# V of every batch from float32 W1, and batch 2's x and half of its z turned by VectorE, in an attention and two-layer kernel on one core

## The chip, the cores and the metric

The program runs on one core of a Trainium2 chip. Its engines are TensorE (PE in the rows; PEld is its weight loads), VectorE (DVE), ScalarE (ACT) and GpSimd (POOL); SyncE (SP) only issues transfers here. The metric is the device time of one execution in microseconds, as the median of several.

## The reference

```python
# x: 8 batches, 8 heads, 512 tokens, 64;  state: 8, 8, 32, 64
xread = softmax(x @ state.T / 8) @ state      # every token reads the state
sread = softmax(state @ x.T / 8) @ x          # the state reads the tokens
a = concat([xread, sread], axis=2)            # 544 tokens of 512 for each batch, 4352 in all
h = a @ w_in                                  # 512 -> 1024
s = h * softmax(h)
z = (s - mean(s)) / sqrt(var(s) + 1e-6) * g_ln
y = z @ w_out                                 # 1024 -> 512
o = y @ w3
out = (o * sigmoid(1.702 * o)) @ w4           # 512 -> 2048 -> 512
```

## The kernel before, in words

**Stages.** The first stage, up to about 440 us, does the attention, the layer with softmax and norm, and w_out, for 8 batches of 512 tokens; the 256 tokens read by the states follow as a ninth, short batch. The second stage multiplies by w3, the third by w4, both in a seven-product block scheme, and together they last to the end.

**How a product is made exact enough.** Most products are three matmuls of rounded parts: high times high, high times low, low times high (`mm3`, L421 to L424, type float32r). A "split" of a tile writes its high part (a rounding copy, L457) and its low part (a subtraction, L458). A few products are single float32 matmuls: the transposes, the scores (L571), the reads (L633) and some of the V below (L671).

**V.** Instead of reading the state and then multiplying by w_in, the kernel multiplies the state of each batch by w_in first: V = state @ W1, four tiles of 128x512 in a batch (two groups g of four heads, two halves f of 1024 columns). The tokens of the batch then take attention weights times V (L763). Batches 0 and 1 make V in `state_w1`: for each tile two float32 matmuls, one for each pair of heads, each with 64 columns of the turned state `stT` as weights and 512 columns of W1 moving; ScalarE rounds the result (`vhi`, L675), VectorE subtracts (`vlo`, L676). Batches 2 to 7 are taken two at a time (`DIRECT`, `state_w1_both`): the states of a pair are split (`sthi`, `stlo`), and each of eight products with the split W1 (`W1s`, in the trace `hi_w1s`, `lo_w1s`) is three matmuls of 128 columns by 512. Its result holds half the rows of either batch's tile, so two copies of 64 rows (`v`, L711) bring these together, and `v` is split afterwards (`hi_v`, `lo_v`). So that the halves land on the right partitions, an odd batch of a pair has its two head pairs swapped (`turned`).

**Turning.** x and z have to be turned before they are multiplied. TensorE turns a 512x128 piece by four matmuls with the identity (`x_T`, L543; `z_T`, L827), and the result is copied out of PSUM. The other way is VectorE's transpose of 32x32 blocks, with transfers that put the blocks in place: for x the transfers come first (`x_T_dma`, L529, tile `xb`, then the transpose at L533), for z the transposes come first (`z_turn`, L797, tile `zw`, then the transfers at L806 into `z`). `XD` and `ZB` say from which batch on x, and the second half of z, go this way: both are 3.

**What sets the order.** The program lists steps with their inputs, outputs, a cost for each engine that may do it, and for TensorE a place in its order (`key`). A planner (`Plan.plan`) then goes through them in a modelled time and fixes the order on each engine, and which engine does a step where two may; rows of the program come out in that order, and each engine runs its own in order. Tiles of 128x512 words live in 71 shared slots of kind `s` (22 more from the point where the first stage's own tiles are done).

Of the kernel before, what the change touches and what calls it, by code (L numbers as in the profile page):

```python
# [19 lines left out]
NWIDE = 7  # L20
NRAW = 2
NZ = 2
ZB = 3
XD = 3
AHEAD = 30.092
KF = 11.222
LOOK = 27.436
KR = 1.553
DIRECT = 2
W1S = 20.477  # L30
ATT = -0.491
ZL = 7.738
M1B = -7.631
VST = 25.191
RK = 6
LEAD = 62.849
KEEP = 5
# [306 lines left out]
def attention_solu_gelu(ctx: ExitStack, tc: tile.TileContext, x, state, w1, w2, g_ln, w3, w4, out):  # L344
# [52 lines left out]
    def PE(c):  # L397
        return [("pe", c)]
# [105 lines left out]
    def attention(b):  # L504
# [5 lines left out]
            n_step[0] += 1  # L510
            return base + (n_step[0] - 1) * SLOT / steps[0]

        both = b >= DIRECT
        turned = both and b % 2
        xt = {}
        load_x(b, 0)
        if not turned:
            load_state(b)
        for j in range(1, NP):
            load_x(b, j)  # L520

# [43 lines left out]
        def scores(g):  # L565
            p = tl("m", [P, 512], F32, f"psc{b}_{g}")

            def go(e):
                for i in range(2):
                    jj = i ^ turned  # L570
                    e.matmul(p()[64 * i:64 * i + 64, :], stT[b]()[:, g, 64 * jj:64 * jj + 64], xt[2 * g + jj](),  # L571
                             start=True, stop=True)

            do(PE(.9), go, [stT[b], xt[2 * g], xt[2 * g + 1]], [p], key())
# [51 lines left out]
        def read_s():  # L626
            p = tl("m", [P, 512], F32, f"psr{b}")

            def go(e):
                for g in range(G):  # L630
                    for c in range(C):
                        for hl in range(HG):
                            e.matmul(p()[NS * hl:NS * hl + NS, g * D:(g + 1) * D],  # L633
                                     e2k[g]()[:, c, NS * hl:NS * hl + NS],
                                     xn[b, 2 * g + (hl // 2 ^ turned)]()[:, c, hl % 2, :],
                                     start=(c == 0), stop=(c == C - 1))

            do(PE(1.55), go, [e2k[0], e2k[1]] + [xn[b, j] for j in range(NP)], [p], key())
            sr = tl("t", [P, G, 2, D], F32, f"sr{b}")
            for g in range(G):  # L640
                do(DVE(.26), lambda e, g=g: e.tensor_scalar(
                    sr()[:, g], p()[:, g * D:(g + 1) * D].unsqueeze(1).to_broadcast([P, 2, D]),
                    r2[g]()[:, 1:2], None, op0=ALU.mult), [p, r2[g]], [sr])
            p2 = tl("m", [P, 512], F32, f"psrT{b}")

            def go2(e):
                for g in range(G):
                    e.transpose(p2()[:, g * P:(g + 1) * P], sr()[:, g].rearrange("p a d -> p (a d)"), ident)

            do(PE(.22), go2, [sr], [p2], key())  # L650
            for q in range(2):
                for a in range(2):
                    def go3(e, q=q, a=a):
                        pv = p2()[:, 0:G * P].rearrange("p (j a n) -> p j a n", a=2, n=NS)
                        o = xs[q]()[64 * a:64 * a + 64, :, b * NS:(b + 1) * NS]
                        if turned:
                            for j in range(2):
                                copy(e, o[:, j], pv[64 * a:64 * a + 64, 2 * q + 1 - j, a, :])
                        else:
                            copy(e, o, pv[64 * a:64 * a + 64, 2 * q:2 * q + 2, a, :])  # L660
                    c = 1 + bool(turned)
                    do([("act", .11 * c), ("dve", .13 * c)], go3, [p2], [xs[q]])

        def state_w1(g, f):
            p = tl("m", [P, 512], F32, f"pv{b}_{g}_{f}")
# [10 lines left out]
            do(DVE(.6), lambda e: e.tensor_tensor(lo(), p(), hi(), op=ALU.subtract), [p, hi], [lo])  # L676
            V[b, g, f] = (hi, lo)

        def state_w1_both():


            hi = tl("s", [P, G, 4, 64], F32R, f"sthi{b}")
            lo = tl("s", [P, G, 4, 64], F32R, f"stlo{b}")
            for i in range(2):
                st = stT[b + i]

                def part(t, i=i):
                    return t()[:, :, 1:3, :] if i else t()[:, :, 0:4:3, :]

                def src(st=st):  # L690
                    return st().rearrange("p g (j n) -> p g j n", j=2)

                do([("act", .29), ("dve", .2)], lambda e, part=part, src=src: copy(e, part(hi), src()), [st], [hi])
                do([("pool", .68), ("dve", .33)], lambda e, part=part, src=src: e.tensor_tensor(
                    part(lo), src(), part(hi), op=ALU.subtract), [st, hi], [lo])
            for f in range(2):
                for g in range(G):
                    v = [tl("s", [P, 512], F32, f"v{b + i}_{g}_{f}") for i in range(2)]
                    for jj in range(2):
                        p = tl("m", [P, 512], F32, f"pv{b}_{g}_{f}_{jj}")  # L700

                        def go(e, p=p, g=g, f=f, jj=jj):
                            wh, wl = W1s[2 * g + jj, f]
                            at = [t()[:, g, 2 * jj:2 * jj + 2, :].rearrange("p i n -> p (i n)") for t in (hi, lo)]
                            mm3(p(), *at, wh(), wl(), True, True)

                        do(PE(.65), go, [hi, lo, *W1s[2 * g + jj, f]], [p], key())
                        for side in range(2):
                            t = v[side ^ jj]
                            r = slice(64 * side, 64 * side + 64)  # L710
                            do([("act", .48), ("dve", .6)], lambda e, t=t, p=p, r=r: copy(e, t()[r, :], p()[r, :]),  # L711
                               [p], [t])
                    for i in range(2):
                        V[b + i, g, f] = split(v[i], f"v{b + i}_{g}_{f}", None)

        x_T(0)
        x_T(1)
        if not turned:
            state_T(b)
        e0 = scores(0)  # L720
        x_T(2)
        x_T(3)
        e2_T(0, e0)
        e1 = scores(1)
        n_step[0] += 1
        if both and not turned:
            load_state(b + 1)
            state_T(b + 1)
        e2_T(1, e1)
        read_s()  # L730
        if both and not turned:
            n_step[0] -= 1
            steps[0] = VST
            state_w1_both()
        if not both:
            for f in range(2):
                for g in range(G):
                    state_w1(g, f)


    n_tiles = {b: C for b in range(B)}
# [473 lines left out]
            prepare_up(k, q, (160, 230, 310)[n])  # L1215
    attention(0)
    for b in range(B):
        if b + 1 == DIRECT:
            for f in range(2):
                for k in range(KD):  # L1220
                    W1s[k, f] = split(W1[k, f], f"w1s_{k}_{f}", b * SLOT + W1S + 2 * (k + KD * f))
        if b + 1 < B:
            attention(b + 1)
        for i in range(C):
            step = SLOT / C if b < B - 1 else SLOT / 6
            last[b] = mlp1(b, i, b * SLOT + M1B + i * step if b else M1A + i * M1S)
        if b == B - 1:
            key = b * SLOT + C * SLOT / 6
            for j in range(KD // 2):
                xs2.append(split(xs[j], f"xs{j}", key - 3, (2, NX)))  # L1230
            for i in range(n_tiles[B]):
                last[B] = mlp1(B, i, b * SLOT + (C + i) * SLOT / 6)
# [77 lines left out]
```

## Time and profile before

| | |
|---|---|
| median of 3 runs | 1126.65 us (1126.53 to 1130.48) |
| the profiled execution | 1126.07 us |
| its span, first to last instruction | 1124.3 us |
| TensorE busy | 1080.0 us, 96% |
| VectorE busy | 825.2 us, 73% |
| ScalarE busy | 637.8 us, 57% |
| GpSimd busy | 258.7 us, 23% |
| mean granted TensorE clock | 0.992 |

The profiled execution is 1.8 us longer than its span and 0.6 us under the median. Matmuls are pipelined: the duration of a row runs on into the next matmul's, so what a matmul costs on TensorE is read from the distance of two starts.

### The profile page before, as it was taken

The page shows a single profiled execution, that of the slowest core. Times are in us where ns is not written, and L with a number is a line of the kernel's source. Part 1 is how long each engine was busy: PE and PEld are TensorE (multiplying, and loading weights), DVE is VectorE, ACT ScalarE, POOL GpSimd, SP SyncE. Part 2 cuts the span into 40 slices and gives each one's busy share as a digit, 9 for nine tenths or more (in the row PEclk, how much of TensorE's full clock was granted, in tenths as well). Part 3 has the DMA queues.
Part 4 walks back from the last instruction along what each step waited for, and adds up shares of the span by engine and source line. Part 5 has one row for each costly group of instructions (what it writes and reads, how often), then busy time and mean ns, then how long its engine had stood idle before and what let it go on. Part 6 is the DMA issues. An engine that isn't in the chain of part 4 may idle for free.

```text
span 1124.3 us, 21689 instructions
## 1 busy us (share of the span) xinstructions
PE 1080.0 (96%) x8055; PEld 976.9 (87%) x8055; DVE 825.2 (73%) x1398; ACT 637.8 (57%) x1171; POOL 258.7 (23%) x218
## 2 busy tenths in 40 slices
PE   6798999799899999999999999999999999999998
PEld 2466677577677889999999999999999999999998
DVE  6999878988989746628757755634388888788874
ACT  6686756866868546547666656545244444344341
POOL 3865443743746701301111000000000000000000
PEclk8899999999999999999999999999999999999999
DMA  8214234568673569998667657559944254344431
GB/s 242 67 39 113 78 70 135 165 126 177 187 162 87 158 153 365 334 374 276 230 233 242 237 204 257 179 209 398 383 145 125 64 170 150 101 144 151 134 93 57
DMA packets 233082, 202.78 MB, mean 180 GB/s; under 512 B 128784, under 2 KB 174864, under 8 KB 232976
## 3 DMA queue, kind: packets, MB, share of 16 engines
q1 hardware_dynamic: 232880, 201.26, 57.3%
q8 instruction: 63, 1.03, 0.4%
q14 instruction: 43, 0.35, 0.1%
q10 hardware_dynamic: 96, 0.13, 0.1%
HBM read 113.25 MB, written 82.84 MB: 174 GB/s over the span
## 4 chain that ended last, share of the span: by engine, by line
PE 75%; DVE 13%; issue 3%; SPq 3%; POOL 3%; DMA 2%; ACT 1%; DVEq 0%; POOLq 0%; ACTq 0%
PE psum L1098 9%; PE psum L1100 9%; PE psum L1099 9%; PE psum L1010 9%; PE psum L1011 9%; PE psum L1012 9%; PE psum L422 5%; PE psum L423 5%; PE psum L424 4%; DVE w_w L449 1%; DVE w_w L444 1%; SPq L529 1%; POOL lo_w3s L458 1%; DVE w_w L447 1%; DVE u L775 1%
## 5 line engine op out<-in xcount | busy, mean ns | idle before, releaser
L1098 PE MATMUL psum<-w4r,hi_g 128*128 128x256 f32 x896 | 251.8, 281 | 1.6 <-DVE oc L1109 1.6
L1100 PE MATMUL psum<-w4r,lo_g 128*128 128x256 f32 x896 | 251.6, 281 | 0.0
L1099 PE MATMUL psum<-w4r,hi_g 128*128 128x256 f32 x896 | 251.6, 281 | 0.0
L1098 PEld LDWEIGHTS psum<-w4r,hi_g 128*128 128x128 f32 x896 | 169.1, 189 | 1.8 <-ACT hi_g L463 1.8
L1100 PEld LDWEIGHTS psum<-w4r,lo_g 128*128 128x128 f32 x896 | 169.3, 189 | 0.0
L1099 PEld LDWEIGHTS psum<-w4r,hi_g 128*128 128x128 f32 x896 | 169.0, 189 | 0.0
L463 ACT CAST hi_g<-a_g 128x512 fp32r<-128x512 f32 x124 | 75.4, 620 | 127.3 <-DVE a_g L880 87.1
L451 POOL TENSOR_TENSOR w_w<-w_w,raw_w 128x512 uint32<-128x512 uint32 x48 | 68.9, 1441 | 284.1 <-DVE w_w L449 206.1
L1022 DVE TENSOR_TENSOR c<-psum,u 128x512 f32<-128x512 f32 x64 | 44.1, 689 | 98.0 <-PE psum L1012 63.7
L422 PE MATMUL psum<-zhi,hi_w 128*128 128x512 f32 (+1 forms) x288 | 113.9, 395 | 1.3 <-DVE zlo L835 0.6
L424 PE MATMUL psum<-zhi,lo_w 128*128 128x512 f32 (+1 forms) x288 | 109.9, 382 | 0.0
L957 DVE TENSOR_TENSOR lo_g<-a_g,hi_g 128x512 fp32r<-128x512 f32 x128 | 84.0, 685 | 19.9 <-PE psum L1099 7.1
L994 ACT ACTIVATE t<-c 128x512 f32<-128x512 f32 x96 | 60.5, 632 | 50.0 <-DVE c L1022 49.9
L957 DVE TENSOR_TENSOR lo_g<-gr,hi_g 128x512 fp32r<-128x512 f32 x104 | 71.0, 685 | 11.8 <-ACT hi_g L463 9.2
L423 PE MATMUL psum<-zlo,hi_w 128*128 128x512 f32 (+1 forms) x208 | 78.3, 376 | 0.2
L463 ACT CAST hi_g<-gr 128x512 fp32r<-128x512 f32 x104 | 61.8, 618 | 28.4 <-PE psum L1099 14.4
L422 PEld LDWEIGHTS psum<-zhi,hi_w 128*128 128x128 f32 x288 | 54.2, 188 | 17.3 <-issue 4.1
L424 PEld LDWEIGHTS psum<-zhi,lo_w 128*128 128x128 f32 x288 | 54.1, 188 | 11.8 <-DVE lo_w L458 0.4
L1010 PE MATMUL psum<-hi_x,w3r_1h 128*128 128x256 f32 x224 | 63.1, 282 | 1.2 <-ACT u L1017 1.2
L1011 PE MATMUL psum<-lo_x,w3r_2h 128*128 128x256 f32 x224 | 63.1, 282 | 0.0
L1010 PE MATMUL psum<-hi_x,w3r_2h 128*128 128x256 f32 x224 | 63.0, 281 | 0.0
L1011 PE MATMUL psum<-lo_x,w3r_3h 128*128 128x256 f32 x224 | 63.0, 281 | 0.0
(261 smaller groups left out, 3101.9 us busy)
## 6 DMA issues: line engine op xcount, KB each, us to landing
g<-t SPq DMA_DIRECT2D x136, 256.0 KB, 3.4
gr<-g SPq DMA_DIRECT2D x136, 256.0 KB, 3.4
w4r<-w4k SPq DMA_DIRECT2D x56, 256.0 KB, 5.2
raw_w<-in_moe_w_in SPq DMA_DIRECT2D x24, 512.0 KB, 6.0
raw_w<-in_moe_w_out SPq DMA_DIRECT2D x24, 512.0 KB, 4.2
xb<-scr SPq DMA_DIRECT2D x34, 256.0 KB, 6.3
scr<-x SPq DMA_DIRECT2D x16, 512.0 KB, 3.6
out<-oc SPq DMA_DIRECT2D x32, 256.0 KB, 3.8
```

What stands on the lines that cost most here:

```text
L422: nc.tensor.matmul(o, lhi, rhi, start=first, stop=False)
L423: nc.tensor.matmul(o, lhi, rlo, start=False, stop=False)
L424: nc.tensor.matmul(o, llo, rhi, start=False, stop=last)
L451: do(POOL(1.23), lambda e: e.tensor_tensor(u(), u(), raw()[:, :, 0], op=ALU.add), [w, raw], [w], key=due)
L463: e.copy(o, i)
L957: do(DVE(.68), lambda e: e.tensor_tensor(flat_(lo), flat_(t), flat_(hi), op=ALU.subtract), [t, hi], [lo], key=due)
L1010: nc.tensor.matmul(o, wh()[:, k, cut], hi()[:, k, :], start=first and not mi + k, stop=False, **OPEN)
L1011: nc.tensor.matmul(o, wh()[:, k, cut], lo()[:, k, :], start=False, stop=False, **OPEN)
L1012: nc.tensor.matmul(o, wl()[:, k, cut], hi()[:, k, :], start=False, stop=bool(mi and k), **OPEN)
L1098: nc.tensor.matmul(o, hi()[:, mi, cut], wt[:, 0], start=first, stop=False, **OPEN)
L1099: nc.tensor.matmul(o, hi()[:, mi, cut], wt[:, 1], start=False, stop=False, **OPEN)
L1100: nc.tensor.matmul(o, lo()[:, mi, cut], wt[:, 0], start=False, stop=2 * j + mi == NM - 1 and u == 1, **OPEN)
```

## The change

V of all batches is made by `state_w1`: two float32 matmuls for each tile, a rounding copy, a subtraction. `state_w1_both` and the swapping of head pairs go, and each batch loads and turns its own state. `XD` and `ZB` become 2, so the four pieces of batch 2's x, and the second half of its z, are turned by VectorE and transfers. The split of W1 into `W1s` is listed just ahead of batch 7 instead of ahead of batch 2's first half, with the due time that goes with it; the last, short batch (L754) still uses it.

```diff
-ZB = 3
-XD = 3
+ZB = 2
+XD = 2
...
-DIRECT = 2
...
-VST = 25.191
...
-        both = b >= DIRECT
-        turned = both and b % 2
...
-        if not turned:
-            load_state(b)
+        load_state(b)
...
-                    jj = i ^ turned
-                    e.matmul(p()[64 * i:64 * i + 64, :], stT[b]()[:, g, 64 * jj:64 * jj + 64], xt[2 * g + jj](),
+                    e.matmul(p()[64 * i:64 * i + 64, :], stT[b]()[:, g, 64 * i:64 * i + 64], xt[2 * g + i](),
...
-                        if turned:
-                            for j in range(2):
-                                copy(e, o[:, j], pv[64 * a:64 * a + 64, 2 * q + 1 - j, a, :])
-                        else:
-                            copy(e, o, pv[64 * a:64 * a + 64, 2 * q:2 * q + 2, a, :])
+                        copy(e, o, pv[64 * a:64 * a + 64, 2 * q:2 * q + 2, a, :])
...
-        def state_w1_both():
...
-        if not turned:
-            state_T(b)
+        state_T(b)
...
-        if both and not turned:
-            load_state(b + 1)
-            state_T(b + 1)
         e2_T(1, e1)
         read_s()
-        if both and not turned:
-            n_step[0] -= 1
-            steps[0] = VST
-            state_w1_both()
-        if not both:
-            for f in range(2):
-                for g in range(G):
-                    state_w1(g, f)
+        for f in range(2):
+            for g in range(G):
+                state_w1(g, f)
...
-        if b + 1 == DIRECT:
+        if b + 1 == B:
             for f in range(2):
                 for k in range(KD):
                     W1s[k, f] = split(W1[k, f], f"w1s_{k}_{f}", b * SLOT + W1S + 2 * (k + KD * f))
```

Line numbers of the changed kernel are lower: 671 becomes 660, 458 becomes 456, 676 becomes 665, 827 becomes 770. Three places show the order of the program's rows. The first is TensorE's, where the V of batch 2 begins, among the z products of batch 0 (`zhi`, `hi_w`) and transposes of its z (`u`). Before:

```order
L827 MATMUL psum<-ident,u_0_705 128x128
L827 MATMUL psum<-ident,u_1_732 128x128
L827 MATMUL psum<-ident,u_2_761 128x128
L827 MATMUL psum<-ident,u_3_814 128x128
L422 MATMUL psum<-hi_w1s_0_482,sthi_934 128x512
L423 MATMUL psum<-lo_w1s_0_604,sthi_934 128x512
L424 MATMUL psum<-hi_w1s_0_482,stlo_976 128x512
L422 MATMUL psum<-zhi_4_1022,hi_w_4_1162 128x512
```

And of the change (`stT_831` is batch 2's turned state, the four `w_w` are float32 tiles of W1):

```order
L660 MATMUL psum<-w_w_2_0_380,stT_831 64x512
L660 MATMUL psum<-w_w_3_0_384,stT_831 64x512
L770 MATMUL psum<-ident,u_0_917 128x128
L770 MATMUL psum<-ident,u_1_1008 128x128
L770 MATMUL psum<-ident,u_2_1040 128x128
L770 MATMUL psum<-ident,u_3_1253 128x128
L660 MATMUL psum<-w_w_0_1_401,stT_831 64x512
L660 MATMUL psum<-w_w_1_1_414,stT_831 64x512
```

Three float32r matmuls for half a tile of two batches have become pairs of float32 matmuls for a whole tile of one. The second place is VectorE's, where batch 2's V is finished; before, among the block transposes of batch 3's x (`xT`) and the softmax of batch 2 (`z_2_1`):

```order
L533 STREAM_TRANSPOSE xT_2_1314<-xb_2_1255 128x512
L465 CAST hi_v_0_0_1323<-v_0_0_1194 128x512
L600 TENSOR_REDUCE z_2_1_1325<-s_2_1_1103 128x16
L601 TENSOR_SCALAR z_2_1_1325<-z_2_1_1325 128x16
L602 RECIPROCAL z_2_1_1325<-z_2_1_1325 128x16
L780 TENSOR_SCALAR sml_3_1172<-sml_3_1172 128x1
L465 CAST hi_v_1_0_1341<-v_1_0_1281 128x512
L458 TENSOR_TENSOR lo_v_1_0_1344<-v_1_0_1281,hi_v_1_0_1341 128x512
```

And of the change:

```order
L528 STREAM_TRANSPOSE xT_3_1351<-xb_3_1321 128x512
L665 TENSOR_TENSOR vlo_0_0_1385<-psum,vhi_0_0_1379 128x512
L665 TENSOR_TENSOR vlo_1_0_1398<-psum,vhi_1_0_1391 128x512
L778 SCALAR_TENSOR_TENSOR zlo_0_1402<-psum,g_sb,zhi_0_1396 128x512
L665 TENSOR_TENSOR vlo_0_1_1410<-psum,vhi_0_1_1404 128x512
L665 TENSOR_TENSOR vlo_1_1_1419<-psum,vhi_1_1_1412 128x512
```

All four subtractions of a batch's V now stand on VectorE, with one input in PSUM. The third place is GpSimd's, in the first 60 us, where the low parts of W1 are made. Before:

```order
L458 TENSOR_TENSOR lo_w1s_0_536<-w_w_0_0_336,hi_w1s_0_479 128x512
L603 TENSOR_TENSOR s_0_1_393<-s_0_1_393,z_0_1_524 128x512
L451 TENSOR_TENSOR w_w_2_1_464<-w_w_2_1_464,raw_w_2_1_328 128x512
L451 TENSOR_TENSOR w_w_3_1_489<-w_w_3_1_489,raw_w_3_1_390 128x512
L610 TENSOR_TENSOR alo_1_584<-aT_1_565,ahi_1_571 128x512
L458 TENSOR_TENSOR lo_w1s_0_604<-w_w_1_0_360,hi_w1s_0_482 128x512
```

And of the change:

```order
L456 TENSOR_TENSOR lo_w1s_0_536<-w_w_0_0_336,hi_w1s_0_479 128x512
L597 TENSOR_TENSOR s_0_1_393<-s_0_1_393,z_0_1_524 128x512
L449 TENSOR_TENSOR w_w_2_1_464<-w_w_2_1_464,raw_w_2_1_328 128x512
L449 TENSOR_TENSOR w_w_3_1_489<-w_w_3_1_489,raw_w_3_1_390 128x512
L604 TENSOR_TENSOR alo_1_584<-aT_1_565,ahi_1_571 128x512
L456 TENSOR_TENSOR lo_w1s_0_604<-w_w_1_0_360,hi_w1s_0_482 128x512
```

Nothing moved here: the planner puts the split of W1 where it was, although the step is listed later.

## Rows read from the trace of the kernel before

**Rows 1.** Busy time by stretch: us, each engine (instructions), granted clock, DMA, GB/s

```profile
60.00:130.00 70.00, 62.27 (x346) 43.50 (x345) 66.52 (x123) 55.57 (x105) 42.47 (x38) 1.00 0.34 92
130.00:180.00 50.00, 49.43 (x296) 38.76 (x295) 34.93 (x67) 29.00 (x60) 15.93 (x16) 1.00 0.35 86
180.00:220.00 40.00, 35.59 (x221) 26.51 (x221) 39.08 (x70) 29.02 (x57) 26.68 (x23) 1.00 0.40 108
220.00:280.00 60.00, 57.40 (x326) 43.88 (x325) 48.62 (x91) 39.31 (x78) 26.64 (x24) 1.00 0.75 168
280.00:320.00 40.00, 34.60 (x216) 25.98 (x215) 38.26 (x63) 32.32 (x60) 25.89 (x21) 1.00 0.67 192
320.00:440.00 120.00, 119.84 (x658) 97.32 (x657) 83.02 (x146) 72.97 (x139) 46.23 (x39) 1.00 0.59 169
440.00:1124.00 684.00, 677.53 (x5725) 676.74 (x5723) 465.44 (x757) 340.37 (x600) 37.99 (x25) 1.00 0.61 206
```

**Rows 2.** Groups of TensorE's instructions, 0 to 440 us: busy, mean ns, idle before

```profile
L422 PE MATMUL psum<-hi_v,ahi 128*128 128x512 f32 x96 | 39.5, 411 | 3.4 <-DVE xs L465 2.6 <-DVE u L775 0.9
...
L422 PE MATMUL psum<-hi_w1s,sthi 128*128 128x512 f32 x24 | 11.0, 457 | 5.8 <-DVE zlo L835 2.5 <-DVE sr L641 2.1 <-ACT v L463 0.6
L621 PE MATMUL psum<-ident,e2t 128*128 128x128 f32 x64 | 10.4, 287 | 10.7 <-ACT e2t L583 10.7
```

**Rows 3.** TensorE's timeline, 59 to 65 us: start, length, line, tiles, count

```profile
59.34 1.08 PE L671 MATMUL psum<-w_w,stT 128*64 128x512 f32 x4
60.35 0.66 PE L543 MATMUL psum<-ident,xn 128*128 128x128 f32 x4
60.94 1.08 PE L671 MATMUL psum<-w_w,stT 128*64 128x512 f32 x4
61.95 0.44 PE L555 MATMUL psum<-ident,S 128*128 128x128 f32 x2
...
64.04 0.60 PE L543 MATMUL psum<-ident,xn 128*128 128x128 f32 x4
64.39 0.47 PE L422 MATMUL psum<-vhi,ahi 128*128 128x512 f32 x1
```

**Rows 4.** TensorE's timeline, 97 to 102 us

```profile
97.90 0.40 PE L422 MATMUL psum<-hi_w1s,sthi 128*128 128x512 f32 x1
...
98.60 0.39 PE L422 MATMUL psum<-zhi,hi_w 128*128 128x512 f32 x1
...
100.84 0.60 PE L827 MATMUL psum<-ident,u 128*128 128x128 f32 x4
101.20 0.48 PE L422 MATMUL psum<-hi_w1s,sthi 128*128 128x512 f32 x1
...
101.99 0.39 PE L422 MATMUL psum<-zhi,hi_w 128*128 128x512 f32 x1
```

**Rows 5.** Instructions of tiles vlo and v: shortest/median/longest ns, first and last start

```profile
L676 DVE TENSOR_TENSOR vlo<-psum,vhi x8: 645/684/693, 35.3 to 64.1; 128x512 fp32r<-128x512 f32 x8
...
L463 ACT COPY v<-psum x47: 562/581/592, 98.8 to 311.9; 64x512 f32<-64x512 f32 x47
...
L458 POOL TENSOR_TENSOR lo_v<-v,hi_v x17: 1272/1308/1762, 113.2 to 344.0; 128x512 fp32r<-128x512 f32 x17
L458 DVE TENSOR_TENSOR lo_v<-v,hi_v x7: 679/969/1783, 115.2 to 346.4; 128x512 fp32r<-128x512 f32 x7
L465 DVE CAST hi_v<-v x3: 379/417/1533, 112.7 to 308.4; 128x512 fp32r<-128x512 f32 x3
```

**Rows 6.** Groups of VectorE's instructions, 0 to 440 us

```profile
L797 DVE STREAM_TRANSPOSE zw<-u 128x512 f32<-128x512 f32 x20 | 13.8, 693 | 8.1 <-POOL u L786 5.4 <-DMA xn<-in_x 2.0 <-DMA z<-zw 0.7
L533 DVE STREAM_TRANSPOSE xT<-xb 128x512 f32<-128x512 f32 x20 | 13.4, 688 | 0.0
```

**Rows 7.** Instructions of tile lo_w1s, as in rows 5

```profile
L458 POOL TENSOR_TENSOR lo_w1s<-w_w,hi_w1s x8: 1287/1304/1478, 32.5 to 58.8; 128x512 fp32r<-128x512 f32 x8
```

**Rows 8.** SyncE's queue of transfers, 28 to 175 us: start, length, line, tiles, count

```profile
34.81 1.97 SPq L500 DMA_DIRECT2D S<-in_state  x4
75.91 12.02 SPq L436 DMA_DIRECT2D raw_w<-in_moe_w_out  x4
88.01 5.43 SPq L529 DMA_DIRECT2D xb<-in_x  x8
```

More of the change, by code (lines that the diff above doesn't have):

```diff
@@ L634, in go @@
                                      e2k[g]()[:, c, NS * hl:NS * hl + NS],
-                                     xn[b, 2 * g + (hl // 2 ^ turned)]()[:, c, hl % 2, :],
+                                     xn[b, 2 * g + hl // 2]()[:, c, hl % 2, :],
                                      start=(c == 0), stop=(c == C - 1))
@@ L655, in go3 @@
                         o = xs[q]()[64 * a:64 * a + 64, :, b * NS:(b + 1) * NS]
-                        if turned:
-                            for j in range(2):
-                                copy(e, o[:, j], pv[64 * a:64 * a + 64, 2 * q + 1 - j, a, :])
-                        else:
-                            copy(e, o, pv[64 * a:64 * a + 64, 2 * q:2 * q + 2, a, :])
-                    c = 1 + bool(turned)
-                    do([("act", .11 * c), ("dve", .13 * c)], go3, [p2], [xs[q]])
+                        copy(e, o, pv[64 * a:64 * a + 64, 2 * q:2 * q + 2, a, :])
+                    do([("act", .11), ("dve", .13)], go3, [p2], [xs[q]])
         def state_w1(g, f):
@@ L677, in state_w1 @@
             V[b, g, f] = (hi, lo)
-        def state_w1_both():
[L682 to L695, printed above, removed]
-            for f in range(2):
-                for g in range(G):
[L698 to L714, printed above, removed]
         x_T(0)
         x_T(1)
-        if not turned:
-            state_T(b)
+        state_T(b)
         e0 = scores(0)
@@ L725, in attention @@
         n_step[0] += 1
-        if both and not turned:
-            load_state(b + 1)
-            state_T(b + 1)
         e2_T(1, e1)
         read_s()
-        if both and not turned:
-            n_step[0] -= 1
-            steps[0] = VST
-            state_w1_both()
-        if not both:
-            for f in range(2):
-                for g in range(G):
-                    state_w1(g, f)
+        for f in range(2):
+            for g in range(G):
+                state_w1(g, f)
     n_tiles = {b: C for b in range(B)}
```

## The prediction

> **What bounds the kernel now.** I read the busy time by stretch first. From 320 us on TensorE is busy all the time: 119.84 of 120 us up to 440, then 677.53 of 684 [rows 1]. Nothing in those last two stages is edited, so the end comes when TensorE has got through the first stage. There it does wait: from 60 to 320 us the five stretches leave 7.7, 0.6, 4.4, 2.6 and 5.4 us idle, 20.7 together, and the large ones are those in which VectorE is full, 66.5 of 70, 39.1 of 40 and 38.3 of 40 us [rows 1]. The granted clock is 1.00 in each of them, its upper level, so a matmul's price doesn't change inside the part that is edited. The groups of TensorE's instructions then say where it waits: 10.7 us before the transposes of the exponentials, 5.8 before the products of W1's split halves with the states, 3.4 before the products that use the finished V of a pair [rows 2]. So the time is TensorE's work plus its waits in the first stage, and the change touches both.
>
> **The change on TensorE.** A float32 pair for one tile of V takes 1.01 us, from its start to that of the next instruction: 59.34 to 60.35 and 60.94 to 61.95 [rows 3]. Six batches (2 to 7) of four tiles make 24 pairs, 24.2 us. They replace 24 triples of float32r matmuls (three pairs of batches, eight products each). A triple takes 0.70 us among other triples, 97.90 to 98.60, and 0.79 behind transposes, 101.20 to 101.99 [rows 4]; so 16.8 to 19.0 us go, and I take 17.5. The same 0.09 us may now be paid by the triple behind each pair, 0 to 2.2 us; I take 1.1. V therefore adds 24.2 + 1.1 - 17.5 = 7.8 us, between 24.2 - 19.0 = 5.2 and 26.4 - 16.8 = 9.6.
>
> Batch 2's x no longer comes over TensorE: four groups of four transposes, each between 0.35 us (64.04 to 64.39) and 0.59 (60.35 to 60.94) [rows 3], 1.4 to 2.4 us, I take 1.9. Four groups of z transposes go too, 0.36 us each (100.84 to 101.20) and perhaps the 0.09 behind them [rows 4], 1.4 to 1.8 us, I take 1.6. TensorE's sum is 7.8 - 1.9 - 1.6 = +4.3 us, with bounds of 5.2 - 4.2 = +1.0 and 9.6 - 2.8 = +6.8.
>
> One rule speaks for a far larger price. The trace shows the two matmuls of a pair together in 1.01 us [rows 3], where one float32r matmul takes 0.70 / 3 = 0.23 [rows 4]. The Trainium skill, "FP8 and Floating Point Precision", section TensorE Precision Notes, says that true float32 makes four passes through the array. With four passes of 0.23 each and no overlap, 48 matmuls would cost 44.8 us and the sum would be 44.8 - 17.5 - 3.5 = +23.8 us, about 1150. The row disagrees with the second half of that: two matmuls of 64 columns share the time of one. I go by the row.
>
> **The change off TensorE.** VectorE gets 24 subtractions from PSUM at 0.684 us [rows 5], 16.4 us, four block transposes of x at 0.688 and four of z at 0.693 [rows 6], 5.5 us. It loses the seven `lo_v` it did, at a median of 0.97, and three `hi_v` at 0.42 [rows 5], 8.1 us. The order of the changed program also hands seven more two-input steps (low halves of weights, scalings of u) back to GpSimd, which has lost 17 `lo_v`; at `lo_v`'s 0.97 that is another 6.8 us. Net 21.9 - 8.1 - 6.8 = +7 us; with 0.68 to 1.78 for the fourteen steps that leave [rows 5] it is between -4 and +11. ScalarE loses 47 copies of 64 rows at 0.58 us [rows 5], 27 us, and GpSimd 17 times 1.31 [rows 5], 22 us, of which the seven come back. Neither is full in any stretch [rows 1], so this costs and gives nothing by itself; it counts through the waits.
>
> SyncE issues 32 more transfers, at 5.43 / 8 = 0.68 us each [rows 8], 22 us of its queue. Those of x stand, in the changed order, ahead of the third weight tile of w_out, for which the queue of before did nothing from 36.8 to 75.9 us [rows 8]: this gap hides them. Behind that wait, batch 2's x would come with what is now batch 3's at 88 us, some 20 us late, and its scores would be late next. The sixteen of z stand behind the stores of batch 1's result and ahead of w3's raw tiles and batch 5's x; 11 us of delay there meet nothing that TensorE needs within a batch. Price zero; cover as named.
>
> W1 is not split later, although the step is listed later: the order is the same, and the low halves are made at 32 to 60 us as now [rows 7]. So the 16 slots of W1's halves stay in use from there, and the 8 of float32 W1 stay too, until batch 7's V. This can delay only what waits for slots, the weights of the second stage. That stage waits 684 - 677.5 = 6.5 us in all now, and the 120 us before it hardly at all [rows 1]; so I take 0, with 0 to 3 (half of that stage's waits again) as bounds.
>
> **The waits.** Two things pull against each other. The V products no longer need a split state, two copies from two PSUM tiles and a split by GpSimd that takes at least 1.27 us [rows 5]; 5.8 + 3.4 = 9.2 us of TensorE's idle stand at such products now [rows 2]. Most of it ends on VectorE steps that stay (the low halves of z, the reads, copies), so I let half go: -4.6. Against it VectorE's +7 lies in a stage that has it full for 150 of 260 us [rows 1]; that share of it, 4.0 us, reaches TensorE. The sum is about nothing, with -9.2 (all such waits vanish) and +11 (all VectorE work is passed on) as bounds.
>
> So 1126.07 + 4.3 = 1130.4 against the profiled execution, which lies 0.6 under the median: **1131 us**.
>
> **Rivals.**
>
> The waits win. V's shorter way is worth the whole 9.2 us, and GpSimd's fewer steps speed VectorE up: `lo_v` there, with both inputs in SBUF, takes 0.68 to 1.78 us while `vlo`, with one input in PSUM, takes 0.645 to 0.693 [rows 5]. Some 15 fewer such steps on GpSimd at the 0.3 us between shortest and median give VectorE 4.5 us, of which 2.6 reach TensorE by the same share. 1126.65 + 4.3 - 9.2 - 2.6 = 1119. It is faster from 4.3 us of saved waits on, and measurably (0.5%, 5.6 us, is what this kernel's measurement can tell) from 9.9 on. The Trainium skill, "SBUF — State Buffer", section Who interferes with whom, says that a VectorE step with two SBUF inputs and a GpSimd step that reads SBUF lock each other out, and one with a single SBUF input doesn't; the spread of the two rows agrees. Against the rival stands that its waits end mostly on steps that stay. Chance 0.18.
>
> VectorE becomes the bound. Each batch's four subtractions stand in its queue in a block, each behind ScalarE's rounding, and what is queued behind them are the low halves of z and the row maxima for which TensorE and ScalarE wait. If all of the +7 to +11 reaches TensorE, the time is 1131 + 3 to 1131 + 11, some 1138 in the middle. For it speaks VectorE at 95 to 98% in three stretches; against it that ScalarE and GpSimd become lighter. The order is also made anew from batch 1 on, and a wait may open anywhere. Chance 0.25.
>
> The change holds more memory than it says, since W1's halves don't wait for batch 7: weights come late, +3, 1134. Chance 0.05, as the later stretches hardly wait now.
>
> Float32 pairs don't overlap among float32r products as they do among transposes: about 1150. Chance 0.02, since the rows of both kinds are at hand.
>
> **How the numbers follow.** The forecast (TensorE's sum, waits level, 1127 to 1135) has 0.5. Faster than 1121.0 takes about half of the first rival, 0.10. Slower than 1132.3 takes nearly all of the second, the two small ones and the forecast's upper quarter, 0.40; the rest, 0.50, lies within 0.5%. The range 1121 to 1141 leaves out the lower half of the first rival and the top of the second with the last.
>
> **What would show it.** TensorE's timeline should have 24 more float32 pairs at 1.01 us apart from the next start, between about 85 and 330 us, and no `sthi` products; the first stage should end some 4 us later, and the stretches after it be the same length. VectorE's busy time up to 440 us should be a few us higher, ScalarE's some 25 lower, GpSimd's some 15 to 20 lower. The idle before the V products should shrink, and idle before the products with zlo or the transposes of exponentials should grow by as much. The prediction is wrong if TensorE's idle from 60 to 320 us leaves 12 to 32 us, if a pair costs other than 1.0 to 1.1 us, or if waits appear behind 440 us.

## The result, and the profile after

The changed kernel takes **1133.22 us** (median of 6 runs, 1132.33 to 1134.39); the kernel before took 1125.68 us beside it (6 runs, 1123.66 to 1130.48). The ratio is 1.0063, with a 95% interval of 1.0042 to 1.0083. The forecast was 1131 with a range of 1121 to 1141; the time lies in the range, but the 0.63% is just past the 0.5% that bounded "no change": what came is "slower", to which the prediction gave 0.40, and not "within 0.5%", to which it gave 0.50. Of 31 more executions of the kernel before, the nine with a mean granted clock of 0.985 to 0.988 took 1129.2 to 1132.7 us, the others, with 0.989 to 0.992 as in the profiled one, 1124.7 to 1128.6. The profiled execution took 1132.84 us, its span is 1131.0, 6.7 more than before.

Busy time by stretch, in the columns and stretches of [rows 1]:

```profile
60.00:130.00 70.00, 61.58 (x323) 43.02 (x322) 60.91 (x114) 44.49 (x85) 40.03 (x35) 0.88 0.35 92
130.00:180.00 50.00, 49.59 (x293) 35.80 (x292) 36.75 (x73) 25.54 (x47) 12.56 (x13) 1.00 0.31 61
180.00:220.00 40.00, 38.11 (x231) 26.37 (x230) 35.95 (x65) 27.14 (x53) 21.28 (x19) 1.00 0.58 140
220.00:280.00 60.00, 58.19 (x324) 41.76 (x324) 50.74 (x93) 36.85 (x71) 25.82 (x23) 1.00 0.77 185
280.00:320.00 40.00, 35.54 (x212) 23.82 (x211) 39.31 (x68) 25.40 (x48) 22.76 (x18) 0.91 0.56 161
320.00:440.00 120.00, 117.94 (x619) 91.62 (x618) 79.69 (x141) 66.36 (x124) 41.48 (x36) 1.00 0.59 158
440.00:1131.00 691.00, 684.21 (x5779) 683.02 (x5777) 470.92 (x766) 346.27 (x610) 37.74 (x25) 1.00 0.62 208
```

Three things are to be seen. TensorE is idle for 8.4, 0.4, 1.9, 1.8 and 4.5 us from 60 to 320, 17.0 in all (before 20.7); but 2.1 us of idle are new at 320 to 440, where there was 0.2. From 60 to 440 us that is 19.1 us, where it was 20.9. The granted clock, 1.00 in every one of these stretches before, is 0.88 in the first and 0.91 in the fifth. And behind 440 us nothing has changed: 691 - 684.2 = 6.8 us idle against 6.5. So the loss is made before 440 us, as forecast; the first product with w3 starts at 444.8 us instead of 438.4, 6.4 later.

Groups of TensorE's instructions, 0 to 440 us, in the columns of [rows 2]:

```profile
L420 PE MATMUL psum<-vhi,ahi 128*128 128x512 f32 x128 | 52.4, 409 | 0.0
L660 PE MATMUL psum<-w_w,stT 128*64 128x512 f32 x128 | 38.8, 677 | 1.7 <-ACT xs L461 0.7 <-POOL w_w L449 0.6 <-ACT zhi L776 0.4
L770 PE MATMUL psum<-ident,u 128*128 128x128 f32 x176 | 29.9, 293 | 9.4 <-POOL u L729 4.1 <-DVE zlo L778 3.8 <-ACT e2t L577 1.4
L615 PE MATMUL psum<-ident,e2t 128*128 128x128 f32 x64 | 10.7, 293 | 8.9 <-ACT e2t L577 7.0 <-DVE zlo L778 1.9
L642 PE MATMUL psum<-ident,sr 128*128 128x128 f32 x16 | 3.4, 297 | 5.4 <-DVE sr L635 5.4
```

The 9.2 us that stood before the products with V and with the split states [rows 2] are down to 1.7 before the pairs and 0.4 before the products with `vlo`. The waits before the transposes of z are 9.4 us and those before the transposes of the states' reads (`sr`) 5.4, where these two groups had 2.8 and 3.3 before.

**What work and what waits.** Since the clock changes too, I separate the two by starts, not by busy time. Each matmul of a trace is given its undisturbed price from start to next start (0.231 us for 512 columns at float32r, 0.118 for 256, 1.01 for a pair of V or of scores, 0.10 for a transpose, 0.0165 for a small product of the reads); whatever the next start comes later than that, up to 440 us, is counted as waiting, and this includes time lost to a lower clock. The gain in span less the gain in waiting is then the gain in work. The kernels are those of the experiments below; waiting in the kernel before is 65.5 us. The method is good to about 1 us, since a lone instruction behind one of another kind costs up to 0.1 us more than it does among its like, and some matmul records are missing.

| kernel | span against before | waiting against before | work, by difference | work by the prediction's rows |
|---|---|---|---|---|
| the change | +6.7 | +2.0 | +4.7 | +4.3 |
| V alone | +6.5 | -0.6 | +7.1 | +7.8 |
| turning alone | -0.6 | +3.1 | -3.7 | -3.5 |
| x alone | +2.5 | +5.2 | -2.7 | -1.9 |
| second half of z alone | +7.5 | +9.9 | -2.4 | -1.6 |
| V of batches 2 to 5 alone | -1.7 | -6.7 | +5.0 | +5.2 |
| the change, batch 7's V early | +4.1 | +0.2 | +3.9 | +4.3 |
| the triples of before twice | +5.2 | -11.2 | +16.4 | +16.8 |

The work comes out as the rows said each time, to about 1 us. What varies is the waiting.

Two things belong to this table. Each row is one execution, the profiled one. By the medians, each against the kernel before of its own group, V alone is 7.0 us slower, turning alone 0.8, x alone 2.2, half of z alone 4.9, batch 7's V early 4.9 and the triples twice 3.9, and V of batches 2 to 5 alone is 0.7 faster. And "waiting" isn't idle time: in the change it grew by 2.0 us, while TensorE's idle time from 60 to 440 us fell by 1.8. So most of what grew, some 4 us by difference, is time that matmuls took longer at the lower clock.

### The profile page after: what moved, and what is told of

Its sections match the earlier page's. It is cut to its first block, busy times and chain, and to the rows that moved or that the text cites. A ratio compares the mean times of both kernels' runs of the same rounds, so it can differ in the third digit from the quotient of the medians.

```text
span 1131.0 us, 21654 instructions
## 1 busy us (share of the span) xinstructions
PE 1089.3 (96%) x8047; PEld 969.3 (86%) x8047; DVE 824.1 (73%) x1404; ACT 611.7 (54%) x1112; POOL 238.6 (21%) x203
## 4 chain that ended last, share of the span: by engine, by line
PE 79%; DVE 11%; DMA 3%; SPq 2%; issue 2%; ACT 2%; POOL 0%; DVEq 0%; ACTq 0%; POOLq 0%
PE psum L1041 9%; PE psum L1042 9%; PE psum L1043 9%; PE psum L953 9%; PE psum L954 9%; PE psum L955 9%; PE psum L420 6%; PE psum L422 5%; PE psum L421 5%; PE psum L660 2%; SPq L749 2%; DVE w_w L442 1%; DVE w_w L447 1%; DMA raw_w<-in_moe_w_in 1%; PE psum L770 1%
## 5 line engine op out<-in xcount | busy, mean ns | idle before, releaser
L449 POOL TENSOR_TENSOR w_w<-w_w,raw_w 128x512 uint32<-128x512 uint32 x48 | 69.7, 1457 | 288.3 <-DVE w_w L447 194.5
L420 PE MATMUL psum<-zhi,hi_w 128*128 128x512 f32 (+1 forms) x288 | 116.3, 404 | 0.2
L421 PE MATMUL psum<-zlo,hi_w 128*128 128x512 f32 (+1 forms) x192 | 72.6, 378 | 0.0
L953 PE MATMUL psum<-hi_x,w3r_0h 128*128 128x256 f32 x224 | 63.1, 282 | 0.1
L954 PE MATMUL psum<-lo_x,w3r_1h 128*128 128x256 f32 x224 | 63.0, 281 | 0.0
```

Source lines behind the costliest of these rows:

```text
L420: nc.tensor.matmul(o, lhi, rhi, start=first, stop=False)
L421: nc.tensor.matmul(o, lhi, rlo, start=False, stop=False)
L449: do(POOL(1.23), lambda e: e.tensor_tensor(u(), u(), raw()[:, :, 0], op=ALU.add), [w, raw], [w], key=due)
L953: nc.tensor.matmul(o, wh()[:, k, cut], hi()[:, k, :], start=first and not mi + k, stop=False, **OPEN)
L954: nc.tensor.matmul(o, wh()[:, k, cut], lo()[:, k, :], start=False, stop=False, **OPEN)
```

## The experiments

Twelve kernels ran in three groups, each beside the kernel before, whose median was 1126.57 us in the first group, 1127.28 in the second and 1125.79 in the third. The theories have names in the expectations. In short: work (a matmul's price reaches the end, and the waits stay), clock (the lower clock of 78 to 95 us is what the turning costs), VectorE's queue (its order at 69 to 90 us sets the pace there), and place (V is cheap where TensorE waits and dear where it doesn't).

**The two halves of the change.** V of all batches from float32 W1, with x and z turned as before:

```diff
# of the change
-ZB = 2
-XD = 2
+ZB = 3
+XD = 3
```

> V of every batch from float32 W1, while batch 2's x and z go over TensorE as before. Theory 1, the time is TensorE's work with level waits: the V part alone adds 7.8 us (5.2 to 9.6), so about 1133 to 1134 where before has 1125.7, and some 3.5 us more than the change had if the turning part gives that back. Theory 2, the price lies in what VectorE and the transfers got with batch 2's x and z (waits and a lower granted clock at 73 to 95 us): V alone costs 0 to 2 us, 1126 to 1128.

Measured: 1133.52 us, ratio 1.0048 (1.0030 to 1.0065). Then the turning alone, on the kernel before, and its two parts apart:

```diff
# of before: turn_alone has both, x_alone the second, z_alone the first
-ZB = 3
-XD = 3
+ZB = 2
+XD = 2
```

> The kernel before with batch 2's x and half of its z turned by VectorE and transfers. Theory 1: 3.5 us less work on TensorE, so 1122 (1121.5 to 1123). Theory 2: the waits and the half clock at 73 to 95 us come with this part, so 5 to 8 us slower, 1131 to 1134.

> The kernel before with batch 2's x alone turned by VectorE. Theory 1: 1.9 us less, 1124 (1123.2 to 1124.4). Theory 2, in the form that x's block transposes stand in VectorE's queue ahead of the low halves of z: 3 to 6 us slower, 1129 to 1132, with TensorE waiting before z's transposes at 73 to 95 us.

> The kernel before with half of batch 2's z alone turned by VectorE. Theory 1: 1.6 us less, 1124 (1123.8 to 1124.4). Theory 2: little is lost here, since z of batch 2 is turned after 150 us; 1125 to 1127.

Measured: both 1127.36 us, ratio 0.9997 (0.9981 to 1.0012); x alone 1128.74, ratio 1.0013 (0.9999 to 1.0028); z alone 1131.42, ratio 1.0026 (1.0008 to 1.0043), in its profiled run 1133.54, the longest of its runs. V alone came as theory 1 said. The turning came as neither did (1122, or 1131 to 1134), nor did z alone (1124, or 1125 to 1127); x alone lies just under what theory 2 gave it. So V carries the loss, and the turning gives nothing, although it takes 3.5 us of work from TensorE. Alone, its parts are no better, and they don't add up: each edit makes the order anew.

Where the waiting of x alone begins can be read in its VectorE timeline (start, length, line, tiles, count):

```profile
71.09 0.71 DVE L533 STREAM_TRANSPOSE xT<-xb 128x512 f32<-128x512 f32 x1
...
72.42 0.41 DVE L444 TENSOR_SCALAR w_w<-w_w 128x512 f32<-128x512 f32 x1
72.86 1.23 DVE L447 TENSOR_SCALAR w_w<-w_w 128x512 uint32<-128x512 uint32 x1
74.13 1.65 DVE L449 SCALAR_TENSOR_TENSOR w_w<-raw_w,w_w 128x512 uint32<-128x512 uint32 x1
...
76.31 0.73 DVE L835 SCALAR_TENSOR_TENSOR zlo<-psum,g_sb,zhi 128x512 fp32r<-128x512 f32 x1
...
79.42 1.29 DVE L533 STREAM_TRANSPOSE xT<-xb 128x512 f32<-128x512 f32 x2
...
83.91 0.75 DVE L835 SCALAR_TENSOR_TENSOR zlo<-psum,g_sb,zhi 128x512 fp32r<-128x512 f32 x1
```

Two block transposes and the conversion of a weight tile (L444 to L449) stand ahead of the first low half of z, the other two block transposes ahead of the third, and the fourth starts at 83.91 us. In the kernel before, that conversion starts at 81.11 us, behind four low halves. The first of them starts at 77.35, no earlier than here, but the other three follow in one go:

```profile
79.14 2.05 DVE L835 SCALAR_TENSOR_TENSOR zlo<-psum,g_sb,zhi 128x512 fp32r<-128x512 f32 x3
```

TensorE's z transposes need the PSUM tiles that these low halves free. So TensorE waits, in the change as well (its timeline; the idle before a row and its releaser in brackets):

```profile
76.86 0.66 PE L770 MATMUL psum<-ident,u 128*128 128x128 f32 x4 [1.41 <-DVE zlo L778]
78.96 1.97 PE L770 MATMUL psum<-ident,u 128*128 128x128 f32 x8 [1.45 <-ACT e2t L577]
82.28 1.12 PE L770 MATMUL psum<-ident,u 128*128 128x128 f32 x4 [1.35 <-DVE zlo L778]
84.46 1.11 PE L770 MATMUL psum<-ident,u 128*128 128x128 f32 x4 [1.07 <-DVE zlo L778]
87.44 1.12 PE L615 MATMUL psum<-ident,e2t 128*128 128x128 f32 x4 [1.87 <-DVE zlo L778]
89.23 1.97 PE L565 MATMUL psum<-xT,stT 128*64 128x512 f32 x4 [0.68 <-ACT e2k L461]
91.14 0.80 PE L420 MATMUL psum<-zhi,hi_w 128*128 128x512 f32 x1
91.73 0.63 PE L421 MATMUL psum<-zlo,hi_w 128*128 128x512 f32 x1
...
95.57 0.40 PE L421 MATMUL psum<-zlo,hi_w 128*128 128x512 f32 x1
```

From the third row on four transposes last 1.12 us where they lasted 0.66, and the product at 91.73 lasts 0.63 where others last 0.39: the granted clock is at its lower level. The windows say when (columns as in [rows 1]):

```profile
70.00:78.00 8.00, 5.54 (x26) 3.08 (x24) 7.93 (x12) 3.04 (x6) 8.00 (x7) 1.00 0.05 11
78.00:82.00 4.00, 1.97 (x8) 1.57 (x8) 4.00 (x6) 4.00 (x9) 2.43 (x2) 0.56 0.74 244
82.00:86.00 4.00, 2.23 (x8) 1.43 (x8) 3.90 (x7) 4.00 (x8) 1.29 (x1) 0.50 0.01 2
86.00:90.00 4.00, 1.88 (x6) 1.01 (x8) 3.97 (x6) 2.10 (x6) 1.52 (x2) 0.50 0.61 183
90.00:95.00 5.00, 5.00 (x13) 3.10 (x10) 4.13 (x9) 2.96 (x6) 1.56 (x2) 0.50 0.17 65
95.00:100.00 5.00, 5.00 (x21) 3.96 (x21) 4.93 (x4) 2.21 (x5) 4.32 (x4) 0.94 0.46 131
```

Two runs ask whether that clock is the cause, or the queue.

**Clock or queue.** The first gives TensorE more to do in the waits, batch 0's eight groups of z transposes twice (2.9 us of work); the second gives VectorE more, the four block transposes of batch 2's x twice (2.8 us). Neither changes another instruction.

```diff
# z0_twice, of the change
-            for i in range(n_tiles[b]):
+            for i in [*range(n_tiles[b])] * (2 if b == 0 else 1):
# xblocks_twice, of the change
-            do(DVE(.6), lambda e: e.transpose(out=xt[j](), in_=t()...), [t], [xt[j]])
+            def turn(e):
+                for _ in range(2 if b == 2 else 1):
+                    e.transpose(out=xt[j](), in_=t()...)
+            do(DVE(.6), turn, [t], [xt[j]])
```

> The changed kernel with the eight groups of z transposes of batch 0 issued twice; they stand at 72 to 92 us, where TensorE waits for VectorE and its granted clock goes to the lower level. 8 x 0.36 = 2.9 us more work. Theory A (what is lost there is the clock: half speed up to 95 us): a busier TensorE keeps the upper level, 1 to 4 us faster than the change, 1129 to 1132. Theory B (what is lost there is the wait for VectorE, and the clock only stretches work that would have waited): 0 to 3 us slower, 1133 to 1136.

> The changed kernel with each of the four block transposes of batch 2's x issued twice on VectorE, 4 x 0.69 = 2.8 us more there at 69 to 81 us. If VectorE's queue sets the pace of this stretch and nothing later makes up for it, 2 to 3 us more than the change, 1135.5 to 1136.5; if TensorE's work alone sets the end, nothing, 1133.

Measured: z transposes twice 1133.66 us, span 1.0 over the change's (0.4 by the medians). Block transposes twice 1136.09 us, span 3.4 over the change's (2.9 by the medians), nearly all of it there from batch 1's third tile on and kept to the end. VectorE's queue sets the pace at 69 to 90 us, and work added there is passed on whole.

The first run doesn't settle the question of the clock, since TensorE didn't keep the upper level in it. The fall came some 7 us later, by the windows of that run:

```profile
82.00:86.00 4.00, 2.10 (x14) 1.86 (x15) 3.93 (x7) 4.00 (x7) 1.29 (x1) 0.92 0.01 2
86.00:90.00 4.00, 2.01 (x10) 1.21 (x10) 3.93 (x6) 2.28 (x6) 1.29 (x1) 0.50 0.43 145
90.00:95.00 5.00, 5.00 (x12) 2.72 (x11) 4.13 (x10) 3.07 (x8) 1.28 (x1) 0.50 0.24 95
```

What it shows is that the upper level at 78 to 85 us gains nothing: the transposes wait for VectorE there. From 89 us on both runs are at the lower level, and TensorE is full from 90 us on. In the change the scores at 89.23 us take 1.91 us to the next start (1.01 in the kernel before, at 86.86), and the ten products of z behind them, from 91.14 to 95.57, take 4.43 us instead of some 2.4. That is 2.9 us more, an estimate from the distances of starts; in the run with the transposes twice it is 2.7. From there to 180 us TensorE waits less than 0.5 us in all, and a delay of TensorE at 118 us is passed on whole (below: with batch 2's pairs issued twice, 3.4 us of work, all is 3.5 us late). So these 2.9 us probably reach the end as well. No run took the lower clock away here, and this stays argued.

**V's matmuls twice.** The order stays the same; the matmuls of the named batches are issued twice into the same result.

```diff
# pairs_twice, of the change (pairs7_twice: b == 7; pairs24_twice: b in (2, 3, 4))
-                for jj in range(2):
+                for jj in (0, 1, 0, 1) if b >= 2 else (0, 1):
# triples_twice, of before
                             mm3(p(), *at, wh(), wl(), True, True)
+                            mm3(p(), *at, wh(), wl(), True, True)
```

> The changed kernel in its own order, with each float32 pair of batches 2 to 7 issued twice, 24 pairs more. Theory 1 (every pair lies on the path at its row's price, wherever it stands): 24 x 1.01 = 24.2 us more than the change, 1157. Theory 2 (a pair that stands where TensorE waits for VectorE is partly hidden; batches 2, 4 and 6 have theirs in such stretches): a third to a half is swallowed, 1145 to 1149.

> The kernel before in its own order, with each of the 24 float32r triples of V issued twice. Theory 1: 24 x 0.70 to 0.73 = 16.8 to 17.5 us more than before, 1143. Theory 2: these stand among waits (5.8 us of idle just before them), so a third to two thirds is swallowed, 1131 to 1138. The difference of the two runs, each against its own kernel, is what V's matmuls cost the path without a new order: 7 us by theory 1.

Measured: all 24 pairs twice 1147.08 us, span 14.8 over the change's; all 24 triples twice 1131.20, span 5.2 over that of before; both as theory 2 said. A second pair costs less than the 1.01 us of a lone one. TensorE's timeline of the run with batch 7's pairs doubled (told further below) has four pairs in its first row, that of the change two:

```profile
353.50 3.65 PE L660 MATMUL psum<-w_w,stT 128*64 128x512 f32 x16
357.09 0.66 PE L770 MATMUL psum<-ident,u 128*128 128x128 f32 x4
```

```profile
352.29 1.94 PE L660 MATMUL psum<-w_w,stT 128*64 128x512 f32 x8
354.15 0.55 PE L770 MATMUL psum<-ident,u 128*128 128x128 f32 x3
356.34 0.33 PE L770 MATMUL psum<-ident,u 128*128 128x128 f32 x1 [1.64 <-POOL u L729]
```

3.59 us for four less 1.86 for two is 0.86 for each further pair: 24 of them are 20.6 us, of which 14.8 reach the end, 72%. Of the triples' 16.8 us, 5.2 do, 31% (by the medians 67% and 23%): in the kernel before, V stood mostly in time that TensorE had to wait anyway. That made me suspect the place where V now stands. The change is level with before up to batch 6's last tile (its row maximum at 345.3 us against 347.0) and 6 us late behind batch 7's, whose V has moved from 295 to 308 us to 348 to 362.

**Where V stands.** Four runs: batch 7's V made behind batch 6's (v7_early); float32 V for batches 2 to 5 alone, with 6 and 7 a pair as before (v6); and doubled pairs in two places.

```diff
# v7_early, of the change
-        load_state(b)
+        if b != 7:
+            load_state(b)
...
-        def state_w1(g, f):
+        def state_w1(g, f, b=b):
...
-        state_T(b)
+        if b != 7:
+            state_T(b)
...
-        for f in range(2):
-            for g in range(G):
-                state_w1(g, f)
+        if b == 6:
+            steps[0] = 21
+            load_state(7)
+            state_T(7)
+        if b != 7:
+            for c in ((6, 7) if b == 6 else (b,)):
+                for f in range(2):
+                    for g in range(G):
+                        state_w1(g, f, c)
# v6, of before
-DIRECT = 2
+DIRECT = 6
```

> The changed kernel with one edit: batch 7's state is loaded and turned, and its four tiles of V are made, right behind those of batch 6 (about 300 to 325 us, where TensorE has 4.5 us idle in 40) instead of at 348 to 362 us, where TensorE is full. The same matmuls are issued in all. Theory P (place: V's matmuls cost little where TensorE waits anyway and their full price where it is full; the change is level with before up to 345 us and loses its 6 us with batch 7): 2 to 4 us faster than the changed kernel, 1129 to 1131, first product with w3 2 to 4 us earlier. Theory Q (work: V's matmuls pass a share of their price to the end wherever they stand): no gain, 1132 to 1135.

> The kernel before with V of batches 0 to 5 from float32 W1 (the constant that says from which batch on states are taken in pairs is 6 instead of 2); batches 6 and 7 stay a pair, x and z are turned as before. Theory P: sixteen of the twenty-four pairs stand among waits and batch 7's V stays with batch 6's, so level with before, 1126 to 1129. Theory Q: sixteen pairs for sixteen triples, two thirds of what V alone cost (6.5 us of span), 1130 to 1132.

> The changed kernel, same order on every engine, with only batch 7's four pairs of V matmuls issued twice: 4.0 us more TensorE work at 348 to 362 us. Theory P: all of it reaches the end, since TensorE is full there, +3.5 to +4 over the changed kernel, 1137. Theory Q: the 60% that all pairs doubled passed on, +2.4, 1135.6. In the run with all pairs doubled the delay grew by only 1.3 us at batch 7; if that holds here too, 1134.5, and P is wrong about where V is dear.

> The changed kernel, same order, with the twelve pairs of batches 2, 3 and 4 issued twice: 12.1 us more work at about 75 to 215 us. Theory P: mostly hidden among the waits, +4 or less over the changed kernel, 1137 at most. Theory Q: 60%, +7.3, 1140.5; the run with all pairs doubled had +8 to +9 behind batch 4.

Measured: batch 7's V early 1130.71 us, ratio to before 1.0038 (1.0026 to 1.0051), span 2.6 under the change's. V of batches 2 to 5 alone 1125.11 us, ratio 0.9985 (0.9974 to 0.9997), span 1.7 under before. Batch 7's pairs twice 1133.43, span 0.6 over the change's (0.2 by the medians). Pairs of batches 2 to 4 twice (they stand at 118 to 217 us) 1140.04, span 7.3 over it (6.8 by the medians), 71% of 10.3 us.

The first two came as "place" said, V of batches 2 to 5 even a little under its 1126; the last two came the other way round, batch 7's pairs under every figure that was given. Batch 7's extra pairs are the cheapest of all, as the wait of 1.64 us behind them in the rows above takes up half of their 3.4 us (it is gone in the doubled run), and 0.9 us are left at the first product with w3 (445.7 us, 444.8 in the change). So TensorE isn't full at 320 to 440 us in the change as it was before, and a price by place doesn't hold.

What does hold is the table: to do batches 6 and 7 by float32 too takes the kernel from v6's span of 1122.6 us to the 1130.8 of V alone; by the table 2.1 us of these 8.2 are work and 6.1 waiting, in which the table counts time at the lower clock. The two traces run level up to 290 us. Behind that, windows of both (columns as in [rows 1]), V alone first:

```profile
290.00:300.00 10.00, 7.60 (x94) 5.11 (x92) 9.79 (x14) 6.04 (x13) 6.64 (x5) 0.99 0.55 148
300.00:303.00 3.00, 0.92 (x4) 0.52 (x6) 3.00 (x8) 1.94 (x7) 3.00 (x3) 0.50 0.98 356
303.00:307.00 4.00, 4.00 (x12) 1.00 (x10) 3.90 (x11) 2.70 (x6) 1.92 (x3) 0.55 0.74 229
```

```profile
290.00:300.00 10.00, 8.15 (x36) 5.84 (x35) 9.83 (x19) 8.21 (x16) 7.92 (x7) 1.00 0.77 238
300.00:303.00 3.00, 2.84 (x12) 1.66 (x10) 3.00 (x4) 2.94 (x7) 1.95 (x3) 1.00 0.66 105
303.00:307.00 4.00, 2.71 (x73) 2.31 (x73) 4.00 (x10) 3.87 (x9) 2.40 (x2) 1.00 0.57 92
```

TensorE's timeline of the change shows the same place, and VectorE's beside it shows why:

```profile
296.73 1.08 PE L660 MATMUL psum<-w_w,stT 128*64 128x512 f32 x4
301.49 0.69 PE L642 MATMUL psum<-ident,sr 128*128 128x128 f32 x2 [3.68 <-DVE sr L635]
302.91 4.91 PE L660 MATMUL psum<-w_w,stT 128*64 128x512 f32 x12 [0.73 <-ACT xs L461]
307.75 0.50 PE L420 MATMUL psum<-zhi,hi_w 128*128 128x512 f32 x1
```

```profile
293.42 0.41 DVE L442 TENSOR_SCALAR w_w<-w_w 128x512 f32<-128x512 f32 x1
293.87 1.42 DVE L445 TENSOR_SCALAR w_w<-w_w 128x512 uint32<-128x512 uint32 x1
295.32 0.69 DVE L447 SCALAR_TENSOR_TENSOR w_w<-raw_w,w_w 128x512 uint32<-128x512 uint32 x1
...
298.26 1.76 DVE L823 TENSOR_TENSOR a_w<-w_w,a_w 128x512 f32<-128x512 f32 x1
...
300.20 0.33 DVE L635 TENSOR_SCALAR sr<-psum,r 128x128 f32<-128x128 f32 x1
```

VectorE is full and prepares weights of the second stage (L442 to L447, L823) ahead of the scaling of the states' reads. TensorE stands at the transposes of `sr` with batch 6's last three tiles of V behind them, waits 3.68 and 0.73 us, and goes on at half the clock: three pairs take 302.91 to 307.75, 1.61 us each. In v6 eight triples for both batches stand at 292 to 307 us between the other products; the waits there are 1.5, 1.4 and 0.3 us, and the clock stays at 1.00. Moving batch 7's V back to this place gained 2.6 us, and the wait of 3.8 us for `sr` stayed. That the weights' place in VectorE's queue makes the wait is read from the trace, not tried.

## Why the prediction was right, and where its sizes were off

**The frame held.** The loss is made before 440 us, the later stretches are unchanged (6.8 us idle against 6.5), and span is work plus waits of TensorE. SyncE's 32 more transfers and W1's slots show no wait of their own: TensorE waits 0.3 us for transfers in all, and from the first product with w3 to the end it is 686.2 us, where it was 685.9.

**TensorE's work held.** Forecast +4.3 us, found +4.7, the same within the method's 1 us. V by itself +7.1 where I had 7.8 (bounds 5.2 to 9.6): pairs that stand back to back cost 0.93 each, not 1.01 (the 1.86 us for two above). That is below the 1.0 to 1.1 us that I had named as a sign of being wrong; V came out a little cheaper for it. Turning -3.7 where I had -3.5. The rival of +24 us is out, but I had put it down to the wrong half. The four matmul records of a pair start two by two, less than 0.01 us apart, and the pair's 0.93 us are four times the 0.231 of one float32r matmul. The Trainium skill, "FP8 and Floating Point Precision", section TensorE Precision Notes, gives true float32 four passes. The trace agrees with that count; what it disagrees with is my "no overlap", as the two matmuls of a pair go through side by side.

**The step that was mis-sized is "the waits", taken as level.** They grew by 2.0 us, and the forecast for the profiled execution, 1130.4, was 2.4 short of the 1132.84 measured: 2.0 of waits and 0.4 of work. Both its parts were off and nearly cancelled again, so that the forecast came this near is partly luck. I let 4.6 of 9.2 us go for V; V alone saved 0.6. That is 6.7 saved in batches 2 to 5, more than I took, and 6.1 given back in batches 6 and 7, at 296 to 308 us and at 356 to 361. For VectorE I added 4.0, from 7 us more of its work. The cost is there in about that size (turning alone: +3.1), but not for that reason: over the whole execution VectorE works 824.1 us, 1.1 less than before. The 24 subtractions came as forecast (all 32 at 0.646 to 0.693 us in the trace after), but besides `lo_v` and `hi_v` other steps left too, to ScalarE and GpSimd. What costs is first the order in its queue at 69 to 90 us, not the sum, and then the lower clock behind it.

**The clock had no term.** The prediction said that the granted clock is 1.00 in the stretches that are edited, "so a matmul's price doesn't change inside the part that is edited". In the change it is 0.88 and 0.91 in two of them. The idle time of TensorE from 60 to 440 us came out 1.8 us lower, so level waits were not far off in the plain sense; the time that the table adds to them is that of matmuls at the lower level, by the estimates above 2.9 us at 89 to 96 us and 2.0 at 303 to 308.

**The signs.** ScalarE is 32 us lower from 60 to 440 us (25 forecast), GpSimd 20 (15 to 20 forecast), but VectorE, which I wanted a few us higher, is 7 lower. The idle before V's products went, as named. What I wanted to grow for it didn't: before the transposes of exponentials it fell from 10.7 to 8.9, before the products with `zhi` and `zlo` from 1.5 to 0.2. It grew before z's own transposes (2.8 to 9.4) and those of `sr`, which I hadn't named. The first stage ends 6.4 us later, not 4. The new pairs were to stand between 85 and 330 us: they begin at 118, and batch 7's stand at 348 to 362. The 2.1 us of idle from 320 to 440 were in no step. The lower clock at 78 to 95 and 300 to 307 us wasn't foreseen either; in the first place it stretched up to 89 us what had to wait for VectorE anyway, and behind that scores and products in a full engine; in the second it costs 2.0 us of V (three pairs at 1.61 instead of 0.93).

**The rivals.** "The waits win" is right for batches 2 to 5 (6.7 of its 9.2 us) and wrong for all six. "VectorE becomes the bound" has the right place at 69 to 90 us, where 2.8 us more on VectorE cost 3.4, and the wrong size.

What stays open: why a doubled pair is nearly free in batches 4 and 7 and nearly whole in 2 and 3 (in the run with all doubled the delay grew by 3.5, 3.7, 0.5 to 1.4, 2.5, 1.9 and 1.2 us from batch 2 to 7) isn't traced wait by wait. And how much of the change's loss is the lower clock isn't shown: no run kept the order and the upper level both.

## What to carry to other kernels

Split a forecast into work and waits by the distance of starts: the work of a replaced group can be had from rows to about a microsecond, and the waits are what to be careful with. Before a step that "only adds work" is costed by its sum on a full engine, look at which step of another engine it is put ahead of in the queue; 2.8 us ahead of the low halves of z cost 3.4, while in the kernel with the turning alone VectorE did 0.5 us less in all and TensorE's waiting still grew by 3. A wait can also cost more than its length: where the clock falls behind it, what comes next is slow although nothing waits any more, and idle time doesn't show that. And an edit made for all batches needn't be worth the same in each: kept for batches 2 to 5 it gives 1125.11 us, 0.9985 of before (0.9974 to 0.9997), the fastest of the kernels here, though by less than the 0.5% that counted as a change.

## What the runs showed of the hardware

TensorE's clock fell to its lower level, 1.2 GHz, in the midst of the edited part: granted 0.56 from 78 to 82 us and 0.50 in the windows from 82 to 95. In the 8 us ahead of that the engine had been busy for 5.5. From 90 to 95 us it was busy all the time and still at the lower level; ten float32r products of 512 columns took 4.43 us there, 0.43 from start to start, where they take 0.23 at the upper one. With more transposes in the waits (6.5 us busy of the 8 from 70 to 78, 2.2 of the 4 behind them) the fall came about 7 us later, at 85 us. In the change it fell again at 300 to 307 us, behind a wait of 3.7 us with a single pair ahead of it. In the kernel before and in v6 the clock is 1.00 at both places, though before TensorE stood once for 2.1 us near 86, longer than any wait of the change from 70 to 79 (1.45 us at most).

A further float32 pair behind another costs 0.86 us, and in bunches 0.90 to 0.93, against 1.01 for one that stands alone among float32r products. A float32r matmul of as many columns takes 0.231, so the pair's two float32 matmuls, with 64 columns of weights each, together cost about four of these.
